# v of the first eight heads loaded in long rows and turned on chip, and the last three second-layer weights loaded in column halves

## The chip, the cores and the metric

The kernel runs on one NeuronCore of a Trainium2 chip. The metric is the device time of one execution in microseconds (us). The work of the core is done by TensorE (PE; its weight loads are listed as PEld), VectorE (DVE), ScalarE (ACT), GpSimd (POOL) and SyncE (SP). The last two are used here almost only to issue DMA transfers, all of which share 16 DMA engines.

## The reference, cut to what matters

An attention over 4 batches of 8 heads (768 positions, head size 64) feeds a soft mixture of experts (3072 tokens of 512 columns, 8 experts of 4 slots, hidden size 1024).

```python
scores = q @ k.T / sqrt(64)              # per batch and head
mask   = causal for retrieval heads; causal and (first 4 keys or last 64) for the others
a      = softmax(where(mask, scores, -1e9))
x      = (a @ v).transpose(0, 2, 1, 3).reshape(3072, 512)

logits = x @ phi                         # 3072 x 32
d = softmax(logits, axis=0); slot_input = d.T @ x        # 32 slots
for e in range(8):
    slot_out[e] = relu(slot_input[e] @ w1[e]) @ w2[e]
c = softmax(logits, axis=1); out = c @ slot_out          # 3072 x 512, float32
```

All inputs are float32 in device memory: q, k and v 6.29 MB each, w1 and w2 16.8 MB each. The output has 6.29 MB.

## The kernel before

**Order of the work.** The program is written with a manual schedule: every engine executes its instructions in the order in which the code issues them. There is no planner. What the code writes first stands first in the queue of its engine.

**Attention, rounds 0 to 15.** The 32 heads are taken as 16 pairs; round n handles pair n (two heads of batch n // 4). One round has six chunks of scores. `scores(n, c)` (L160) multiplies on PE and `exp`s on ACT from PSUM into `pT`. `mask` (L174) multiplies three of the chunks on DVE. `pvmm(n - 1, i)` (L186), which multiplies the exponentials of the pair before with v, stands between the chunks on PE; its products are divided by their sums in `norm` (L196) on DVE. For the pair after this one, `transposes` (L135) turns q and k, 24 transposes of 64x64 each, into PSUM tiles `tpq` and `tpk`; `evac` (L144) copies them to `Tq` (on DVE) and `Tk` (on ACT), and undoes the order in which the rows came. `vfar(n)` (L154) makes on DVE a masked copy of v. Two buffers in PSUM (tag `tr`) serve all transposes in turn: a third waits until the first has been copied away.

**Loads.** Every load casts from float32 to bf16 and is issued by POOL, in the order of the code. `load_qk` (L106) takes q and k so that a partition holds 12 consecutive positions of a head: rows of 12 x 64 floats, 3 KB. `load_v` (L116) puts position p of a block of 128 in partition p, which is the layout that `pvmm` reads: rows of 64 floats. A load of v has four heads and 0.39 MB in bf16. `w_load` (L128) issues the weights in between. A load whose buffer is still in use makes POOL wait; for q and k that ends with the last transpose of the pair that used the buffer before.

**The end of attention and the experts.** The buffers of `w2_5`, `w2_6` and `w2_7` are those of the mask and of `pT`, so these three are loaded only when the last rounds free them (L401 to L441): `w2_5` and `w2_6` whole, `w2_7` in two column halves, left and right. After the last pair the logits, the slot inputs and the first layer follow (L428 to L487). `second(e, xs)` (L507) adds the second layer of expert e to the column halves `xs` of the slots, in two PSUM banks `sp`. Experts 0 to 3 go together, then 4, 5, 6; after that 7 products with zeros keep PE occupied, and `second(7, (0,))` ends the left half:

```python
    second(5, spread=True)
    second(6, spread=True)
    keep_busy(idle, 7)
    second(7, (0,), spread=True)
```

**Outputs.** The tokens are laid out as 24 rows of 128 tokens. `product` (L540) multiplies one row with `slot_out`, and ACT or DVE scales it by the sum of its exponentials. `half_rows` does so for one column half. The left half of rows 0 to 7 (`NL = 8`) is made as soon as the left `slot_out` is there, and written from POOL's queue; then the right half of expert 7 is added, rows 8 to 23 are made whole, and the right half of rows 0 to 7 comes last, both written from SP's queue.

Of the kernel before, what the change touches and what calls it, by code (L numbers as in the profile page):

```python
# [10 lines left out]
F32 = mybir.dt.float32  # L11
BF16 = mybir.dt.bfloat16
# [26 lines left out]
def kernel(  # L39
# [13 lines left out]
    nc = tc.nc  # L53
    P = 128
    B, H, S, D = q.shape
    n_sink, window = int(n_sink), int(window)
    ES = moe_phi.shape[1]
    NE, DM, F = moe_w1.shape
# [11 lines left out]
    xp = ent(tc.tile_pool(name="xp", bufs=2))  # L70
    scp = ent(tc.tile_pool(name="scp", bufs=2, space=PSUM))
    trp = ent(tc.tile_pool(name="trp", bufs=2, space=PSUM))
    pvp = ent(tc.tile_pool(name="pvp", bufs=2, space=PSUM))

    def single(shape, dt, name, tag=None):
        return singles.tile(shape, dt, name=name, tag=tag or name)

    w1s = [single([P, 4, F], BF16, f"w1_{e}") for e in range(NE)]
    w2s = [single([P, 8, DM], BF16, f"w2_{e}") for e in range(NE - 3)] + [None] * 3
    ident = single([P, P], BF16, "ident")  # L80
# [23 lines left out]
    qraw, kraw, qT, kT, vf, pT, pv, xb = {}, {}, {}, {}, {}, {}, {}, {}  # L104

    def load_qk(pairs, order="qk"):  # L106
        b, h, c = pairs[0] // 4, 2 * (pairs[0] % 4), 2 * len(pairs)
        t = raw.tile([P, 2, 2, S], BF16, tag="raw", name="raw")
        for which in order:
# [3 lines left out]
            for x, n in enumerate(pairs):  # L113
                d[n] = t[:, z, x]

    def load_v(m):  # L116
        b, h = m // 2, 4 * (m % 2)
        nc.gpsimd.dma_start(vbs[m % 3].rearrange("p h j d -> p (h j) d")[:, :, :D],  # L118
                            v[b, h:h + 4].rearrange("h (j p) d -> p (h j) d", p=P))

    def vb(n):
        return vbs[n // 2 % 3][:, 2 * (n % 2):2 * (n % 2) + 2]

    w1v = [moe_w1[e].rearrange("(di do) f -> di do f", do=4) for e in range(NE)]
    w2v = [moe_w2[e].rearrange("(fi fo) d -> fi fo d", fo=8) for e in range(NE)]
# [7 lines left out]
            wi[0] += 1  # L133

    def transposes(n, which):  # L135
        src = (qraw if which == "q" else kraw)[n]
        tp = trp.tile([P, 12, 64], BF16, tag="tr", name="tp" + which)
        for s in range(12):
            for hh in range(2):
                po = slice(64 * hh, 64 * hh + 64)  # L140
                nc.tensor.transpose(tp[po, s, :], src[po, 64 * s:64 * s + 64], ident[po, po])  # L141
        return tp

    def evac(n, which, tp):  # L144
        dst = qkT.tile([P, S], BF16, tag="T" + which, name="T" + which)
        o, i = dst.rearrange("c (p s) -> c p s", s=12), tp.rearrange("c s p -> c p s")
        if which == "q":
            nc.vector.tensor_copy(o, i)  # L148
            qT[n] = dst
        else:  # L150
            nc.scalar.copy(o, i)  # L151
            kT[n] = dst

    def vfar(n):  # L154
        h = 2 * (n % 4)
        t = vfp.tile([P, 2, 4, 66], BF16, tag="vf", name="vf")
        nc.vector.tensor_mul(t, vb(n)[:, :, :4, :], fmask[:, h:h + 2])
        vf[n] = t
# [27 lines left out]
    def pvmm(n, i):  # L186
        if i % 3 == 0:
            pv[n] = pvp.tile([P, 3, 2, 65], F32, tag="pv", name="pv")
        for hh in range(2):
            for j in range(i + 1):  # L190
                vv = vb(n) if i - j <= 1 else vf[n]
                o = BLK[j, i]
                nc.tensor.matmul(pv[n][:, i % 3, hh, :], pT[n][:, hh, o:o + 128], vv[:, hh, j, :D + 1],  # L193
                                 start=(j == 0), stop=(j == i))
# [68 lines left out]
    def keep_busy(t, count):  # L263
        for _ in range(count):
            nc.tensor.matmul(t, zero[:, :P], zero, start=True, stop=True)  # L265

    idle = pvp.tile([P, 512], F32, tag="pv", name="idle")
# [52 lines left out]
    for n in range(NP):  # L320
        if n == 0:
            load_qk([2])
            load_v(1)
        elif n == 1:
            load_qk([3])
        elif n == 2 or (n % 2 == 1 and n < 12):
            m = 2 if n == 2 else (n + 3) // 2
            load_qk([2 * m, 2 * m + 1])
            load_v(m)
        w_load(1 + 5 * (n + 1) // 8)  # L330
        if n == 0:
            nc.gpsimd.dma_start(phi, moe_phi.rearrange("(do di) s -> di do s", di=P))
        b, r = n // 4 - 1, n % 4
        last = n - 1

        scores(n, 0)
        if n >= 1:
            for i in range(3):
                pvmm(last, i)
        if b >= 0 and r == 2:  # L340
            logits_mm(b, (0, 1, 2, 3))

        scores(n, 1)
        if b >= 0 and r == 2:
            logits_exp(b)
        if n >= 1:
            norm(last, 0)
        if 0 < n < NP - 1:
            tq = transposes(n + 1, "q")
            evac(n + 1, "q", tq)  # L350
        mask(n, 0)
        if b >= 0 and r == 3:
            exp_tokens(b)

        scores(n, 2)
        if n >= 1:
            pvmm(last, 3)
        if n >= 2:
            x_transpose(n - 2)
        mask(n, 1)  # L360

        scores(n, 3)
        if 0 < n < NP - 1:
            tk = transposes(n + 1, "k")
        mask(n, 2)

        scores(n, 4)
        if 0 < n < NP - 1:
            evac(n + 1, "k", tk)
        if n >= 1:  # L370
            pvmm(last, 4)
        if n:
            vfar(n)

        scores(n, 5)
        if n == 0:
            vfar(0)
        if n >= 1:
            pvmm(last, 5)
            norm(last, 1)  # L380
        if b >= 0 and r == 3:
            dispatch_mm(b)
            slot_sum(b)
        if n == 0:
            evac(1, "q", transposes(1, "q"))
            evac(1, "k", transposes(1, "k"))
        if n < 3:
            far_mask(n + 1)
            for h in (2 * n + 2, 2 * n + 3):
                head_mask(h)  # L390
        elif n == 3:
            setup_late()
# [3 lines left out]
    left, right, full = slice(0, 256), slice(256, 512), slice(0, 512)  # L396

    def w_half(e, cs):
        nc.gpsimd.dma_start(w2s[e][:, :, cs], w2v[e][:, :, cs])

    w2s[5] = single([P, 8, DM], BF16, "w2_5", tag="msk")  # L401
    nc.gpsimd.dma_start(w2s[5], w2v[5])
    w2s[6] = ptp.tile([P, 8, DM], BF16, tag="pT", name="w2_6")
    nc.gpsimd.dma_start(w2s[6], w2v[6])


    def bank(t, shape=(P, 512), dt=F32):
# [30 lines left out]
    logits_mm(bl, (0, 1, 2))  # L438
    w2s[7] = ptp.tile([P, 8, DM], BF16, tag="pT", name="w2_7")
    w_half(7, left)  # L440
    w_half(7, right)  # L441
    x_transpose(last, 0, 3)
    x_transpose(last, 3, 6)
    copies(2, 0)
    idle = bank(2)
# [11 lines left out]
    idle = bank(2)  # L457
# [10 lines left out]
    cs = bank(1, (P, 1))  # L468
# [5 lines left out]
    for e4 in range(2):  # L474
        t = xp.tile([P, 2, 512], BF16, tag="xb", name="hs")
# [29 lines left out]
    idle = spt[1][:, 1]  # L505

    def second(e, xs=(0, 1), spread=False):  # L507
        e4, g = e // 4, e % 4
        for fo in range(8):
            c = fo % 4 if spread else g  # L510
            for x in xs:
                nc.tensor.matmul(sp[x][32 * c:32 * c + 32, :], hT[e4][:, fo, 32 * g:32 * g + 32],  # L512
                                 w2s[e][:, fo, 256 * x:256 * x + 256],
                                 start=(e4 == 0 and fo == 0), stop=(e == 7 and fo >= 4))
# [13 lines left out]
        er.append(e)  # L528
        nc.tensor.matmul(rp[:, r:r + 1], e[:ES], ones[:ES], start=True, stop=True)
    V.reciprocal(rrow, rp)  # L530
    second(5, spread=True)
    second(6, spread=True)
    keep_busy(idle, 7)
    second(7, (0,), spread=True)


    NL = 8
    ov = out.rearrange("(p r) d -> p r d", r=24)

    def product(r, o, cs, t):  # L540
        op = bank(t, (P, cs.stop - cs.start))
        nc.tensor.matmul(op, er[r], slot_out[:, cs], start=True, stop=True)  # L542
        if t == 2:
            nc.scalar.activation(o, op, ACT.Copy, scale=rrow[:, r:r + 1])  # L544
        else:
            V.tensor_scalar(o, op, rrow[:, r:r + 1], None, op0=ALU.mult)  # L546

    def half_rows(cs, t0, groups, banks, eng):
        ot, r = single([P, NL, 256], F32, f"oh{t0}", tag=f"w1_{t0}"), 0
        for rows in groups:  # L550
            for _ in range(rows):
                product(r, ot[:, r], cs, banks[r % len(banks)])
                r += 1
            eng.dma_start(ov[:, r - rows:r, cs], ot[:, r - rows:r])  # L554

    V.tensor_copy(slot_out[:, left], sp[0])  # L556
    half_rows(left, 0, (2, 2, 4), (1, 2), nc.gpsimd)
    second(7, (1,), spread=True)
    V.tensor_copy(slot_out[:, right], sp[1])  # L559
    r = NL  # L560
    for z, groups in enumerate(((1, 1, 2), (4,), (4,), (4,))):
        ot, base = single([P, 4, DM], F32, f"ot{z}", tag=f"w1_{4 + z}"), r
        for rows in groups:
            for _ in range(rows):
                if r == NL:
                    for t, cs in ((1, left), (2, right)):
                        product(r, ot[:, 0, cs], cs, t)
                else:
                    product(r, ot[:, r - base], full, (1, 2)[r % 2])
                r += 1  # L570
            nc.sync.dma_start(ov[:, r - rows:r, :], ot[:, r - rows - base:r - base])
    half_rows(right, 2, (4, 4), (1, 2), nc.sync)


# [33 lines left out]
```

The softmax here doesn't subtract the row's maximum and nothing guards it: scores larger than these inputs give would overflow.

## Time and profile before

| | |
|---|---|
| median of three runs | 159.69 us (159.01 to 160.25) |
| the profiled execution | 159.01 us, of which its span is 157.2 us |
| PE, DVE, ACT, POOL busy | 76%, 67%, 70%, 24% of the span |
| read from device memory, written to it | 52.49 MB, 6.29 MB |
| L172, 96 exponentials on ACT | 83.4 us, 923 ns each |
| L151, 16 copies Tk on ACT | 12.9 us, 804 ns each |
| L148, 16 copies Tq on DVE | 15.3 us, 956 ns each |
| L211, 17 copies xT on DVE | 9.0 us, 529 ns each |
| loads of v, 8 of 384 KB | 13.0 us from issue to landing (median) |
| mean granted clock of PE | 0.921 |

Busy shares are means over stages with different limits. In the page's slices, one character stands for a fortieth of the span (3.93 us), and a 9 for 90% or more. A chain line has a start, a duration, and the engine and line that the time went to. In a timeline the brackets give the idle time of the engine ahead of the instruction and what ended it. A wait is put down to the semaphore that came last.

### The profile page before, as it was taken

What the parts mean: (1) busy time and instruction counts of PE and PEld (TensorE: products, weight loads), DVE (VectorE), ACT (ScalarE), POOL (GpSimd) and SP (SyncE); (2) the same over time, 40 slices, a digit from 0 to 9 for tenths busy, and PEclk for the clock granted to TensorE, in tenths of its full rate; (3) what the DMA queues carried; (4) which work ended last, traced back from release to release, by engine and by line L of the source; (5) the groups of instructions that cost most, each with busy time, mean ns of one, the idle gap of its engine ahead of it and who ended that gap; (6) DMA issues with size and microseconds to landing.
All of it is one profiled execution on the core that took longest, in us unless ns stands there. A gap on an engine that the chain in (4) does not pass through costs nothing. (4 is left out here: it accounts for less than half of the span.)

```text
span 157.2 us, 5051 instructions
## 1 busy us (share of the span) xinstructions
PE 119.3 (76%) x2241; PEld 74.8 (48%) x2243; DVE 105.8 (67%) x245; ACT 109.5 (70%) x147; POOL 38.0 (24%) x54
## 2 busy tenths in 40 slices
PE   6757698868597879977978977978897897788000
PEld 2325466545365555655655655645633673344000
DVE  2886459998986878977869979768724410489000
ACT  3286589969799999999898999899242310389000
POOL 7674051900350350250084100001320000040000
PEclk9975559999999999999999999999999998799955
DMA  3999999999999999999999999999999999369995
GB/s 46 165 186 204 169 217 207 192 190 186 219 215 200 186 217 200 185 224 195 188 213 198 191 219 213 217 215 217 215 217 213 219 196 183 44 226 401 404 387 182
DMA packets 36135, 32.85 MB, mean 209 GB/s; under 512 B 26002, under 2 KB 33170, under 8 KB 33810
## 3 DMA queue, kind: packets, MB, share of 16 engines
q0 software_dynamic: 34192, 27.30, 109.8%
q1 hardware_dynamic: 1922, 5.24, 8.7%
q8 instruction: 17, 0.28, 0.7%
q14 instruction: 4, 0.03, 0.1%
HBM read 52.49 MB, written 6.29 MB: 374 GB/s over the span
## 5 line engine op out<-in xcount | busy, mean ns | idle before, releaser
L172 ACT ACTIVATE pT<-sc 128x1024 bf16<-128x1024 f32 (+1 forms) x96 | 83.4, 923 | 9.4 <-PE sc L167 8.9
L167 PE MATMUL sc<-Tq,Tk 64*128 64x256 bf16 (+3 forms) x320 | 36.6, 292 | 13.4 <-ACT Tk L151 9.8
L193 PEld LDWEIGHTS <-pT 128*128 128x128 bf16 x672 | 25.0, 99 | 12.2 <-issue 7.8
L184 DVE TENSOR_TENSOR pT<-pT,msk 128x1024 bf16<-128x1024 bf16 (+1 forms) x48 | 29.4, 640 | 0.2 <-ACT pT L172 0.2
L193 PE MATMUL pv<-vb,pT 128*128 128x65 bf16 x352 | 27.6, 196 | 0.3 <-DVE xb L202 0.3
L193 PE MATMUL pv<-vf,pT 128*128 128x65 bf16 x320 | 25.4, 198 | 0.0
L167 PEld LDWEIGHTS <-Tk 64*128 64x128 bf16 x320 | 11.2, 95 | 22.5 <-ACT Tk L151 13.1
L141 PEld LDWEIGHTS <-raw 64*64 64x64 bf16 x768 | 15.9, 115 | 10.9 <-issue 7.5
L202 DVE TENSOR_TENSOR xb<-pv,rs 128x384 bf16<-128x384 f32 x32 | 17.8, 557 | 1.1
L148 DVE COPY Tq<-tpq 128x768 bf16<-128x768 bf16 x16 | 15.3, 956 | 4.9 <-PE tpq L141 4.6
L111 POOL DMA_DIRECT2D raw<-in_q_dram x10 | 6.4, 639 | 49.5 <-PE tpk L141 48.3
L151 ACT COPY Tk<-tpk 128x768 bf16<-128x768 bf16 x16 | 12.9, 804 | 4.9 <-PE tpk L141 4.9
L201 DVE RECIPROCAL rs<-pv 128x6 f32<-128x6 f32 x32 | 6.2, 195 | 12.5 <-PE pv L193 12.4
L141 PE MATMUL tpk<-ident,raw 64*64 64x64 bf16 x384 | 9.8, 201 | 2.9 <-DMA raw<-in_k_dram 1.5
L118 POOL DMA_DIRECT2D vb<-in_v_dram x8 | 11.6, 1452 | 1.1 <-issue 0.9
L141 PE MATMUL tpq<-ident,raw 64*64 64x64 bf16 x384 | 9.6, 200 | 1.2 <-DMA raw<-in_q_dram 1.2
L210 PE MATMUL tpx<-ident,xb 128*128 128x128 bf16 x96 | 8.1, 218 | 2.0 <-ACT expT L224 1.1
L211 DVE COPY xT<-tpx 128x768 bf16<-128x768 bf16 (+1 forms) x17 | 9.0, 529 | 0.8 <-PE tpx L210 0.8
L544 ACT ACTIVATE oh<-bank,rrow 128x256 f32<-128x256 f32 x8 | 3.5, 474 | 8.7 <-PE bank L542 8.6
L542 PE MATMUL bank<-slot_out,expR 128*128 128x256 bf16 (+1 forms) x33 | 7.9, 323 | 1.7 <-DVE slot_out L556 0.5
L132 POOL DMA_DIRECT2D w<-in_moe_w_dram x12 | 6.6, 556 | 4.3 <-DMA raw<-in_q_dram 2.6
L554 POOL DMA_DIRECT2D out_dram<-oh x3 | 2.2, 737 | 22.4 <-ACT oh L544 22.4
(88 smaller groups left out, 117.2 us busy)
## 6 DMA issues: line engine op xcount, KB each, us to landing
w<-in_moe_w_dram POOLq DMA_DIRECT2D x15, 1024.0 KB, 18.0
vb<-in_v_dram POOLq DMA_DIRECT2D x8, 384.0 KB, 13.0
out_dram<-ot SPq DMA_DIRECT2D x3, 1024.0 KB, 7.7
raw<-in_q_dram POOLq DMA_DIRECT2D x6, 384.0 KB, 10.0
raw<-in_k_dram POOLq DMA_DIRECT2D x6, 384.0 KB, 11.6
w<-in_moe_w_dram POOLq DMA_DIRECT2D x2, 512.0 KB, 21.8
out_dram<-oh SPq DMA_DIRECT2D x2, 512.0 KB, 9.5
raw<-in_k_dram POOLq DMA_DIRECT2D x4, 192.0 KB, 6.9
```

What stands on the lines that cost most here:

```text
L118: nc.gpsimd.dma_start(vbs[m % 3].rearrange("p h j d -> p (h j) d")[:, :, :D], v[b, h:h + 4].rearrange("h (j p) d -> p (h j) d", p=P))
L141: nc.tensor.transpose(tp[po, s, :], src[po, 64 * s:64 * s + 64], ident[po, po])
L148: nc.vector.tensor_copy(o, i)
L151: nc.scalar.copy(o, i)
L167: nc.tensor.matmul(sc[:, hh, at:at + 128 * cnt], kT[n][po:po + 64, j * 128:(j + 1) * 128], qT[n][po:po + 64, i0 * 128:(i0 + cnt) * 128], s ...
L172: nc.scalar.activation(pT[n][:, :, o:o + ln], sc[:, :, :ln], ACT.Exp, scale=scale)
L184: nc.vector.tensor_mul(x, x, m)
L193: nc.tensor.matmul(pv[n][:, i % 3, hh, :], pT[n][:, hh, o:o + 128], vv[:, hh, j, :D + 1], start=(j == 0), stop=(j == i))
L202: nc.vector.tensor_mul(xb[b][:, 3 * half:3 * half + 3, h * D:(h + 2) * D].rearrange("p i (h d) -> p i h d", h=2), pv[n][:, :, :, :64], rs. ...
L210: nc.tensor.transpose(tp[:, i * 128:(i + 1) * 128], xb[b][:, i, hp * 128:(hp + 1) * 128], ident)
L211: nc.vector.tensor_copy(xT[:, hp, i0 * 128:i1 * 128], tp[:, i0 * 128:i1 * 128])
L542: nc.tensor.matmul(op, er[r], slot_out[:, cs], start=True, stop=True)
```

## The change

The change has two parts.

First, v of pairs 0 to 3 (batch 0) is loaded like q and k, in rows of 12 positions, into a tile `vraw` that shares its buffers with `xb`. The new `v_blocks(n)` turns it twice: 24 transposes of 64x64 on PE (as for q and k), a copy `Tv` on ACT that undoes the order of rows, six transposes of 128x128 on PE, and a copy on DVE into the place from which `pvmm` reads. `v_blocks(0)` stands at the end of round 0, ahead of the transposes of pair 1; `v_blocks(1)` to `v_blocks(3)` stand in rounds 1 to 3 between `pvmm(n - 1, 4)` and `vfar(n)`, ahead of `scores(n, 5)`. The other twelve pairs are loaded as before.

Second, `w2_5`, `w2_6` and `w2_7` all come in column halves, first the three left ones and then the three right ones; the left halves of experts 5, 6 and 7 are added first, without the seven products with zeros, and the right ones after the left output rows. `NL` is 12 instead of 8, and `product` takes its engine from the row's number.

```diff
+    vraw = xp.tile([P, 2, 2, S], BF16, tag="xb", name="vraw")
+
     def load_v(m):
         b, h = m // 2, 4 * (m % 2)
+        if m < 2:
+            nc.gpsimd.dma_start(vraw[:, m], v[b, h:h + 4].rearrange("(y h) (p s) d -> (h p) y (s d)", h=2, s=12))
+            return
         nc.gpsimd.dma_start(vbs[m % 3].rearrange("p h j d -> p (h j) d")[:, :, :D],
...
     def transposes(n, which):
-        src = (qraw if which == "q" else kraw)[n]
+        src = vraw[:, n // 2, n % 2] if which == "v" else (qraw if which == "q" else kraw)[n]
...
             nc.scalar.copy(o, i)
-            kT[n] = dst
+            if which == "k":
+                kT[n] = dst
+            return dst
+
+    def v_blocks(n):
+        vT = evac(n, "v", transposes(n, "v"))
+        tp = trp.tile([P, 6, P], BF16, tag="tr", name="tpv")
+        for j in range(6):
+            nc.tensor.transpose(tp[:, j, :], vT[:, 128 * j:128 * j + 128], ident)
+        nc.vector.tensor_copy(vb(n).rearrange("p h j d -> p j h d")[:, :, :, :D], tp.rearrange("p j (h d) -> p j h d", h=2))
...
         if n >= 1:
             pvmm(last, 4)
+        if 0 < n < 4:
+            v_blocks(n)
         if n:
             vfar(n)
 
         scores(n, 5)
         if n == 0:
+            v_blocks(0)
             vfar(0)
...
     w2s[5] = single([P, 8, DM], BF16, "w2_5", tag="msk")
-    nc.gpsimd.dma_start(w2s[5], w2v[5])
+    w_half(5, left)
     w2s[6] = ptp.tile([P, 8, DM], BF16, tag="pT", name="w2_6")
-    nc.gpsimd.dma_start(w2s[6], w2v[6])
+    w_half(6, left)
...
     w_half(7, left)
-    w_half(7, right)
+    for e in (5, 6, 7):
+        w_half(e, right)
...
-    second(5, spread=True)
-    second(6, spread=True)
-    keep_busy(idle, 7)
-    second(7, (0,), spread=True)
-
-
-    NL = 8
+    for e in (5, 6, 7):
+        second(e, (0,), spread=True)
+
+
+    NL = 12
...
-        if t == 2:
+        if r % 2:
             nc.scalar.activation(o, op, ACT.Copy, scale=rrow[:, r:r + 1])
...
     V.tensor_copy(slot_out[:, left], sp[0])
-    half_rows(left, 0, (2, 2, 4), (1, 2), nc.gpsimd)
-    second(7, (1,), spread=True)
+    half_rows(left, 0, (2, 2, 4, 4), (1, 2), nc.gpsimd)
+    for e in (5, 6, 7):
+        second(e, (1,), spread=True)
     V.tensor_copy(slot_out[:, right], sp[1])
...
-    for z, groups in enumerate(((1, 1, 2), (4,), (4,), (4,))):
+    for t, groups in enumerate(((1, 1, 2), (4,), (4,))):
...
-    half_rows(right, 2, (4, 4), (1, 2), nc.sync)
+    half_rows(right, 2, (4, 4, 4), (1, 2), nc.sync)
```

More of the change, by code (lines that the diff above doesn't have):

```diff
@@ L548, in half_rows @@
     def half_rows(cs, t0, groups, banks, eng):
-        ot, r = single([P, NL, 256], F32, f"oh{t0}", tag=f"w1_{t0}"), 0
+        ots = [single([P, n, 256], F32, f"oh{t0 + x}", tag=f"w1_{t0 + x}") for x, n in enumerate((8, NL - 8))]
+        r = 0
         for rows in groups:
             for _ in range(rows):
-                product(r, ot[:, r], cs, banks[r % len(banks)])
+                product(r, ots[r // 8][:, r % 8], cs, banks[r % len(banks)])
                 r += 1
-            eng.dma_start(ov[:, r - rows:r, cs], ot[:, r - rows:r])
+            eng.dma_start(ov[:, r - rows:r, cs], ots[(r - 1) // 8][:, (r - rows) % 8:(r - 1) % 8 + 1])
     V.tensor_copy(slot_out[:, left], sp[0])
-    half_rows(left, 0, (2, 2, 4), (1, 2), nc.gpsimd)
-    second(7, (1,), spread=True)
+    half_rows(left, 0, (2, 2, 4, 4), (1, 2), nc.gpsimd)
+    for e in (5, 6, 7):
+        second(e, (1,), spread=True)
     V.tensor_copy(slot_out[:, right], sp[1])
     r = NL
-    for z, groups in enumerate(((1, 1, 2), (4,), (4,), (4,))):
-        ot, base = single([P, 4, DM], F32, f"ot{z}", tag=f"w1_{4 + z}"), r
+    for t, groups in enumerate(((1, 1, 2), (4,), (4,))):
+        ot, base = single([P, 4, DM], F32, f"ot{t}", tag=f"w1_{4 + t}"), r
         for rows in groups:
             for _ in range(rows):
[L565 to L569, printed above, removed]
+                product(r, ot[:, r - base], full, (1, 2)[r % 2])
                 r += 1
             nc.sync.dma_start(ov[:, r - rows:r, :], ot[:, r - rows - base:r - base])
-    half_rows(right, 2, (4, 4), (1, 2), nc.sync)
+    half_rows(right, 2, (4, 4, 4), (1, 2), nc.sync)
 _INS = ['q', 'k', 'v', 'is_retrieval', 'n_sink', 'window', 'moe_phi', 'moe_w1', 'moe_w2']
```

## The prediction

> **What bounds the kernel now.** I read the page's slices first, then the chain that ended last, then the timelines of the early rounds and of the end, with windows of a microsecond for the DMA rates.
>
> ```profile
> PEclk9975559999999999999999999999999998799955
> DMA  3999999999999999999999999999999999369995
> GB/s 46 165 186 204 169 217 207 192 190 186 219 215 200 186 217 200 185 224 195 188 213 198 191 219 213 217 215 217 215 217 213 219 196 183 44 226 401 404 387 182
> ```
>
> The DMA engines are full until slice 34, empty in a hole at 132 to 138 us, and full again with outputs. The chain shows what fills the hole:
>
> ```profile
> 110.00 21.41 DMA w<-in_moe_w_dram
> ...
> 131.45 0.63 PE bank L512 x16
> ...
> 132.24 2.57 PE bank L265 x6
> 134.80 0.58 PE bank L512 x8
> ...
> 135.41 0.44 DVE slot_out L556
> ```
>
> The 21.41 us are not one transfer but the queue before it. After w2_6 lands, PE runs 2.57 us of zero products, then the left half of expert 7; the left slot_out starts at 135.41. The first output bytes follow 2.8 us later (the windows view has 0 GB/s at 137 to 138 and 172 at 138 to 139), and the last leave at about 155.4. So the end is set by the time of that slot_out plus the writing of 6.29 MB. The compute chain is little behind the data: PE ran expert 5 at 129.82 without a wait for data and waited 1.00 us for expert 6.
>
> The rounds ahead of that are bound by ACT (nearly 100% from 44 us on), except for a few gaps early (timeline, all engines; start, duration, engine, and in brackets the idle time before and what ended it):
>
> ```profile
> 8.32 5.06 ACT L172 ACTIVATE pT<-sc 128x1024 bf16<-128x1024 f32 x6 [1.06 <-PE sc L167]
> ...
> 17.85 0.85 PE L141 MATMUL tpq<-ident,raw 64*64 64x64 bf16 x24 [1.19 <-DMA raw<-in_q_dram]
> ...
> 23.34 0.20 DVE L201 RECIPROCAL rs<-pv 128x6 f32<-128x6 f32 x1 [1.63 <-PE pv L193]
> ...
> 27.68 1.02 ACT L172 ACTIVATE pT<-sc 128x1024 bf16<-128x1024 f32 x1 [0.28 <-PE sc L167]
> ...
> 28.60 0.79 ACT L151 COPY Tk<-tpk 128x768 bf16<-128x768 bf16 x1
> ...
> 29.28 4.21 ACT L172 ACTIVATE pT<-sc 128x512 bf16<-128x512 f32 x5
> ...
> 32.07 0.95 DVE L148 COPY Tq<-tpq 128x768 bf16<-128x768 bf16 x1
> ...
> 33.87 0.57 PE L141 MATMUL tpk<-ident,raw 64*64 64x64 bf16 x24 [1.45 <-DMA raw<-in_k_dram]
> ...
> 41.47 1.02 ACT L172 ACTIVATE pT<-sc 128x1024 bf16<-128x1024 f32 x1 [0.86 <-PE sc L167]
> ```
>
> The reader is to see two waits for data, 1.19 us in round 1 and 1.45 us in round 3. The second is nearly false: the same transposes need the buffer that DVE's Tq copy frees at 33.02, so without the wait for k they could begin 0.85 us sooner and no more. The line at 23.34 is where DVE, having waited for PE, starts the chain that ends in such a Tq copy. The gap of round 4 (0.86 on ACT) is DVE's, not data's.
>
> [...] 163 GB/s at 17 to 20 us, where v moves in 64-element rows, against a mean of 213 with weights alone (92 to 120 us). [...] Here the granted clock is 0.50 from 10 to 23 us, so the first turn is paid at half clock. [...] Tk stands between two exponentials every round.
>
> **The change part by part.**
>
> *v in long rows.* A load of 0.393 MB at 163 GB/s takes 2.41 us, at the 205 GB/s that q, k and weights make together at 24 to 30 us 1.92: twice 0.5 = 1.0 us of DMA time (0.6 to 1.5). POOL's issue falls from 1.42 to about 0.70 us; POOL is idle. This pays only if DMA stays the bound.
>
> *The turns.* v_blocks puts on PE 24 small transposes (0.57 at full clock), on ACT a copy of Tk's shape (0.80), on PE 6 transposes (0.49), on DVE a copy (0.53 as xT's, 0.96 as Tq's). PE waits for ACT in the middle, and behind it on PE stand scores(n,5), for which ACT waits in turn. Taken at round 2: Tk ends 29.39, the v copy about 30.10, the six end 30.62, scores(2,5) 30.78, its exponential 0.63, then exp(3,0) at 31.56 instead of 29.91 (29.28 plus one of 0.63): 1.65 us.
>
> *Turn 0* stands before the transposes of pair 1. v's 24 start at 12.36, end 13.2; ACT is in exponentials until 13.38, copies to 14.18; six at half clock (0.8) to 15.0; k's transposes need the buffer that the DVE copy frees at 15.6 to 16.0, then 0.85, Tk 0.80: scores(1,0) at 17.3 to 17.7 instead of 14.74. +2.8. It hides the q wait of round 1 in full: -1.2.
>
> *Turn 1*: +1.9 (1.7 to 2.3, by the clock); [...] -0.3.
>
> *DVE behind the turns.* The copy (0.53 to 0.96) and vfar (0.43) now come after the six transposes and ahead of rs, xb, fmask, msk, rs, xb, Tq, the transposes of k and scores(n,4). In round 2 that chain began 0.47 before exp(2,0) and now begins 0.02 to 0.45 after it; ACT was already waiting for it (the 0.28), so +0.7. In round 3 it began 0.82 before; now Tq ends at what was 33.9 to 34.3, which takes the place of the data wait: +0.2 (0 to 0.4). In round 4, with setup_late in the chain, it began 1.1 before and ACT already lost 0.86: +1.3 (1.1 to 1.6).
>
> *Turns 2 and 3*: +1.65 each.
>
> Sum until round 4: 2.8 - 1.2 + 1.9 - 0.3 + 0.7 + 1.65 + 0.2 + 1.65 + 1.3 = 8.7 us (7.7 to 10.3). No later round waits for data, so the delay reaches the end of the attention part (110.05) and PE's second product of expert 5: 129.8 + 8.7 = 138.5.
>
> *Halves of w2_5 and w2_6.* At 128 to 132 us, where w2_7's 512 B pieces mix in, 196 GB/s against 213: 5.35 for 4.92 us, +0.4 each (0 to 0.6). POOL issues two more DMAs at 0.89 us; idle. Covered by the compute delay: raw loads wait for PE's transposes, so their issue is late too and DMA runs dry for 1 to 2 us about four times from 32 us on. I put the inputs' end at 140 to 142, before the first output (142.4). If that cover is gone it costs what it is late, up to 2 us.
>
> *Zero products and order of the second products.* 7 x 0.43 of work and the wait for w2_7's left half go. From 138.5 all left halves are there (w2_7 left by about 133): 24 products, 0.95 by the 0.63 of 16, and 0.3 for the last to end, so that without any delay the cast would start at 131.1 instead of 135.41: -4.3. The right half's 24 products come after the left products, another 0.95, with 12 left rows (1.57 MB, 3.9 us) being written meanwhile; full rows are ready about 6 us after the left cast, the left ones are drained at 6.9. No starved start (before, 1.3 us of bytes were lost at 138 to 141): -0.6. Eight more half rows in 1 KB pieces, 1.05 MB at 343 (153 to 155 us) rather than 405 GB/s: +0.5. Two more products and evictions at 0.2 lie beside writing. Tail: -4.4 (-3.8 to -5.0).
>
> **Sum.** +8.7 - 4.4 = +4.3 on the profiled 159.01 us (span 157.2 and 1.8 around it): 163.3. That run is the lowest of three, 0.7 below the median of 159.69; I leave the number as it is, since the three spread over 0.8%. About 1% is what can be told from no change.
>
> **Rivals.**
> - *The DVE copies hide.* If DVE's chain has slack in rounds 2 to 4, 2.2 us go: d = 6.3 with a tail of -4.6 gives 160.7. For it: DVE is at 67%. Against: ACT waits in exactly those places already. 0.16.
> - *Faster: the turns fit into the waits.* If PE and ACT do v's turn wholly in time in which they wait (1.06, 0.71, 1.44, 1.31 us idle on ACT before 35 us), d is about 2 and the left half is ready 2.4 us sooner than now: 156.6. It decides from d below 4.4. For it: PE is at half load and DMA still full at 35 us; earlier q and k help. Against: the waits of ACT in those rounds are partly its own chain, and turns 2 and 3 have none beside them. 0.13.
> - *The clock stays at half.* [...] six more half-speed gaps of 0.3 and slower turns, +2.7: 166.0. For it: the clock fell at 9.8 in just such a round. Against: round 1 is dense once q is there. 0.09.
>
> **How the numbers follow.** The forecast holds 0.62, at 163.3, own range 161.0 to 165.3. Slower by over 1%: 0.60 from it, 0.03 of the DVE rival, 0.09 of the clock: 0.72. Within 1%: 0.02, 0.13 and 0.01 of the fast rival: 0.16. Faster: 0.12. The range, 158.5 to 166.0, takes forecast and DVE rival whole and half the clock's.
>
> **What would show it.** Right: four Tv copies of 0.80 on ACT; no q wait in round 1; exp(4,0) at about 44.4 (now 37.0); the last exponential ending near 118.7; DMA gaps near 33 and 50 us; the left slot_out at 139.8; outputs without a hole after 142.5; span 161.5. Wrong: exp(4,0) before 41.4, or a left slot_out before 135.4, which would make it faster; an input end after 143 would mean that DMA, not the rounds, decides.

## The result and the profile after

The changed kernel takes 164.64 us (median of six, 164.07 to 165.18) against 159.03 for the kernel before on the same chip: a ratio of 1.033, 95% interval 1.029 to 1.037, so 3.3% slower. Medians here and below are of all executions of a kernel; the ratios and their intervals leave out those that ran over 1.5% above its fastest. Of the 5.0 us between the two spans (157.2 and 162.2) the trace makes two parts: the attention rounds end 9.0 us later, and what follows them is 4.0 us shorter. The forecast had 8.7 and 4.4.

The page of the changed kernel (slices: granted clock, share of the DMA engines, GB/s), and then the pieces of its chain of waits at the end:

```profile
PEclk9955576986995999999999999999999999999655
DMA  3999999999996997999999999999999999979995
GB/s 47 161 218 199 183 221 175 179 176 153 218 212 122 188 207 134 187 196 186 187 199 162 180 198 206 216 224 210 210 226 202 192 199 196 177 237 367 410 360 186
```

```profile
138.88 0.80 PE bank L531 x24
...
139.70 0.43 DVE slot_out L574
...
142.64 0.80 PE bank L531 x24
...
143.46 0.43 DVE slot_out L578
```

The DMA engines are no longer full in the middle: slices 12 and 15 have 122 and 134 GB/s, where raw loads (q and k) were issued late. The chain no longer holds a wait for weights. The 24 products of the left halves run at once; the left slot_out starts at 139.70 (forecast 139.8; 135.41 before).

What became of the rounds, in ACT's timeline (brackets: idle time before, and what ended it):

```profile
13.28 0.82 ACT L157 COPY Tv<-tpv 128x768 bf16<-128x768 bf16 x1
...
18.01 1.02 ACT L187 ACTIVATE pT<-sc 128x1024 bf16<-128x1024 f32 x1 [0.70 <-PE sc L182]
...
24.20 0.82 ACT L157 COPY Tv<-tpv 128x768 bf16<-128x768 bf16 x1
26.07 0.60 ACT L187 ACTIVATE pT<-sc 128x512 bf16<-128x512 f32 x1 [1.05 <-PE sc L182]
27.44 1.02 ACT L187 ACTIVATE pT<-sc 128x1024 bf16<-128x1024 f32 x1 [0.77 <-PE sc L182]
...
33.02 0.83 ACT L157 COPY Tv<-tpv 128x768 bf16<-128x768 bf16 x1
34.68 0.60 ACT L187 ACTIVATE pT<-sc 128x512 bf16<-128x512 f32 x1 [0.82 <-PE sc L182]
35.54 2.17 ACT L187 ACTIVATE pT<-sc 128x1024 bf16<-128x1024 f32 x2 [0.26 <-DVE vf L172]
...
44.47 3.56 ACT L187 ACTIVATE pT<-sc 128x1024 bf16<-128x1024 f32 x4 [0.26 <-DVE vf L172]
50.22 1.02 ACT L187 ACTIVATE pT<-sc 128x1024 bf16<-128x1024 f32 x1 [2.19 <-PE sc L182]
```

After the copies Tv of rounds 1 to 3 the next exponential, that of chunk 5, has to wait 0.82 to 1.05 us for PE: its scores stand behind the six transposes, which could start only when Tv was there. And the gap before exp(4,4), the line at 50.22, has grown from 0.86 to 2.19 (exp(n,c) is the exponential of chunk c in round n). The groups of the turn say the same from PE's side (busy, mean ns, idle before):

```profile
L166 PE MATMUL tpv<-ident,Tv 128*128 128x128 bf16 x24 | 2.5, 250 | 5.8 <-ACT Tv L157 5.8
L167 DVE COPY vb<-tpv 128x768 bf16<-128x768 bf16 x4 | 2.2, 558 | 10.4 <-PE tpv L166 10.4
```

PE stood still for 5.8 us waiting for the four copies Tv. That is more than it worked on the 24 transposes of 128x128 (2.5).

The starts of exp(n,0) set the steps of the forecast beside what happened:

| start of | before | changed | later by | forecast | split turns (below) |
|---|---|---|---|---|---|
| exp(1,0) | 15.39 | 18.01 | 2.6 | 2.8 | 2.8 |
| exp(2,0) | 23.84 | 27.44 | 3.6 | 3.2 | 2.3 |
| exp(3,0) | 29.93 | 35.54 | 5.6 | 5.55 | 3.1 |
| exp(4,0) | 37.05 | 44.47 | 7.4 | 7.4 | 3.3 |
| exp(5,0) | 43.72 | 52.69 | 9.0 | 8.7 | 3.8 |
| end of the last exponential | 110.05 | 119.04 | 9.0 | 8.7 | 4.4 |

### The profile page after: what moved, and what is told of

Read it like the earlier page. It is cut to its first block, busy times and chain, and to the rows that moved or that the text cites. A ratio compares the mean times of both kernels' runs of the same rounds, so it can differ in the third digit from the quotient of the medians.

```text
span 162.2 us, 5297 instructions
## 1 busy us (share of the span) xinstructions
PE 123.2 (76%) x2357; PEld 79.7 (49%) x2359; DVE 108.1 (67%) x251; ACT 113.2 (70%) x152; POOL 39.4 (24%) x57
## 5 line engine op out<-in xcount | busy, mean ns | idle before, releaser
L182 PE MATMUL sc<-Tq,Tk 64*128 64x256 bf16 (+3 forms) x320 | 38.0, 303 | 11.0 <-ACT Tk L157 7.7
L208 PEld LDWEIGHTS <-pT 128*128 128x128 bf16 x672 | 25.9, 101 | 12.8 <-issue 8.1
L208 PE MATMUL pv<-vb,pT 128*128 128x65 bf16 x352 | 28.5, 200 | 0.3 <-DVE xb L217 0.3
L208 PE MATMUL pv<-vf,pT 128*128 128x65 bf16 x320 | 26.0, 201 | 0.0
L417 POOL DMA_DIRECT2D w<-in_moe_w_dram x6 | 5.2, 878 | 27.1 <-PE pv L208 25.3
L124 POOL DMA_DIRECT2D vb<-in_v_dram x6 | 8.5, 1422 | 4.3 <-PE pv L208 3.6
L167 DVE COPY vb<-tpv 128x768 bf16<-128x768 bf16 x4 | 2.2, 558 | 10.4 <-PE tpv L166 10.4
L561 ACT ACTIVATE oh<-bank,rrow 128x256 f32<-128x256 f32 x12 | 5.2, 472 | 4.0 <-PE bank L559 3.9
```

Of the source, the lines that this page charges most:

```text
L182: nc.tensor.matmul(sc[:, hh, at:at + 128 * cnt], kT[n][po:po + 64, j * 128:(j + 1) * 128], qT[n][po:po + 64, i0 * 128:(i0 + cnt) * 128], s ...
```

## The experiments

The theory is the forecast's: a turn costs the rounds more than its instructions, since PE waits in its middle and DVE's work comes late after it; the tail gains; DMA time is not what decides. The rivals put the loss into the halved weights, or the cost into the work itself.

**The first part alone.** The first part of the diff on the kernel before, without the second.

```diff
+        if 0 < n < 4:
+            v_blocks(n)
...
     w_half(7, left)
     w_half(7, right)
...
     keep_busy(idle, 7)
```

> The first part of the change alone: v of pairs 0 to 3 in long rows and turned; the weights, products and outputs at the end as before. Theory (the turns delay the rounds, about 9 us, and nothing takes it up later): the second product of expert 5 at 138.8 as in the changed kernel, then 0.63 for expert 6, the seven zero products (1.5 at full clock, 2.6 at half) and 0.3 for expert 7, so the left slot_out at 142 to 143 against 135.4 before: 6.6 to 7.7 us slower, about 166. Rival (the loss lies in the halved weights and in DMA at the end): within 1 us of before, about 159 to 160.

Measured: 1.046 times the kernel before (1.035 to 1.057), 7.3 us slower at its 159.9. That is within the theory's 6.6 to 7.7, though the interval is wider (5.5 to 9.0 us). Where the left slot_out came was not seen: the one profiled execution took 199.19 us, with slower products on PE (two zero products in 0.89 us, 0.54 in the changed kernel; six of them in 3.05, 2.57 in the kernel before), and is not read. The first part is the loss, all of it.

**The second part alone.** `v_blocks`, `vraw` and the case of `load_v` taken out of the changed kernel.

```diff
-        if m < 2:
-            nc.gpsimd.dma_start(vraw[:, m], ...)
-            return
...
-        if 0 < n < 4:
-            v_blocks(n)
```

> The second part of the change alone: w2_5, w2_6 and w2_7 in column halves, no zero products, 12 split rows; v loaded as before. Theory: expert 5 at 129.8 as before, the left slot_out at about 131 to 132 instead of 135.4, left rows written while the right halves end: 3 to 4.5 us faster, about 155. Rival (half columns cost the DMA engines what they bring, at 0.4 to 0.6 us a weight, and the inputs' end near 137 holds the right half back): at most 1 us faster, 158 to 159; if the halves were the loss, slower than 160.

Measured: 157.07 us, ratio 0.987 (0.976 to 0.997): 2.2 us faster by the ratio, less than the 3 to 4.5 of the theory and more than the rival's 1 us at most. Its chain and windows tell why (windows: after the length, busy time of PE, PEld, DVE, ACT and POOL, then clock, DMA share and GB/s):

```profile
115.10 22.10 DMA w<-in_moe_w_dram
...
137.91 0.43 DVE slot_out L560
```

```profile
138.00:139.00 1.00, 0.61 (x2) 0.31 (x2) 0.33 (x1) 0.00 (x0) 0.00 (x0) 0.50 0.75 295
139.00:140.00 1.00, 0.78 (x2) 0.33 (x2) 0.89 (x2) 0.57 (x1) 0.00 (x0) 0.50 0.35 135
140.00:141.00 1.00, 1.00 (x4) 0.43 (x3) 0.90 (x2) 0.81 (x2) 0.00 (x0) 0.50 0.39 145
```

The left slot_out was at 130.11, 5.3 us sooner than before, but the right one stayed at 137.91 (137.88 before): the last right half landed at 137.2, after PE had waited 2.04 us for it. That is the rival's reason, though the gain is larger than it allowed. Most of the 12 left rows were written by 139, and the DMA engines had 135 and 145 GB/s until whole rows came. With nothing late ahead of it, the tail is DMA's, and its gain is what the left rows fill.

**The long rows without the turns.** The loads of v in long rows, ones in place of v of pairs 0 to 3, the end as before.

> The long rows without the turns, the end as before. Left out: v of pairs 0 to 3 is loaded into its tile and not used, ones stand in its place. Theory (two loads of v are 0.5 us of DMA time shorter each, and the inputs decide the end): q of pair 2 comes up to 1 us sooner, and the end is 1.0 us earlier (0.6 to 1.5): about 158. Rival (DMA time is not what decides, the rounds are): no change, 159.0, within 0.3 us.

Measured: 157.56 us, ratio 0.988 (0.980 to 0.995), 2.0 us faster. The chain of waits no longer has a transfer of weights among its last pieces, and PE goes through experts 5 and 6 without a stop:

```profile
128.94 1.84 PE bank L528 x32
...
131.11 2.00 PE bank L280 x6
133.10 0.36 PE bank L528 x8
133.49 0.43 DVE slot_out L572
```

Before, expert 6 waited 1.00 us for its weights. The gain is above the theory's 1.0 (0.6 to 1.5), and the rival's "no change" is out. From 130 us on 0.57 MB of input are still to come, where before it was 0.83 (sums of the windows), about 1.3 us of DMA time by an estimate at 200 GB/s (the windows of before have 190 and 206 at 130 to 132 us). The rounds, which now wait less for q of pair 2 (0.76 on ACT against 1.44), end 1.0 sooner. And of the 1.9 us by which the left slot_out comes sooner in this trace, about 0.8 are zero products and products of expert 7 that ran less at half clock (2.00 and 0.36 us against 2.57 and 0.58; granted clock 0.91 at 132 to 133 us and 1.00 at 133 to 134, against 0.71 and 0.50); that has nothing to do with v. So the long rows by themselves are worth having, and the turns are what they cost; how the 2.0 divide was not separated.

**The turn in two places.** The changed kernel, with the first half of turns 1 to 3 moved up.

```diff
+        if 0 < n < 4:
+            v_first(n)              # 24 transposes, Tv
         if n >= 1:
             pvmm(last, 3)
...
         if 0 < n < 4:
-            v_blocks(n)
+            v_second(n)             # six transposes, copy on DVE
```

> The changed kernel with the turns of pairs 1 to 3 in two places: the 24 transposes and ACT's copy Tv already after scores(n, 2), the six transposes and DVE's copy where they were, so that PE does not stand still between the two halves and ACT has its exponential when Tv ends. Same instructions. Theory (half of a turn's cost is PE waiting for ACT, 1.65 us a turn of which 0.8 is the copy itself): 0.8 less for each of three turns and up to 0.5 less of DVE's lateness: 2.4 to 3.5 us faster than the changed kernel, about 161.5. Rival (the work itself, ACT's 0.8 and DVE's copy, costs it): less than 1 us faster, about 164.

Measured: 160.34 us, ratio 1.003 (0.999 to 1.008) to before, with the same instructions, where the changed kernel has 1.033 (measured in another set of runs): 4.3 us less by the medians, 4.8 by the ratios. More than the 2.4 to 3.5 expected; the rival (the work itself, less than 1 us) is out. ACT's timeline:

```profile
28.63 0.82 ACT L157 COPY Tv<-tpv 128x768 bf16<-128x768 bf16 x1
29.82 1.94 ACT L191 ACTIVATE pT<-sc 128x1024 bf16<-128x1024 f32 x2 [0.37 <-PE sc L186]
...
42.28 2.81 ACT L191 ACTIVATE pT<-sc 128x1024 bf16<-128x1024 f32 x3 [0.86 <-PE sc L186]
45.29 1.02 ACT L191 ACTIVATE pT<-sc 128x1024 bf16<-128x1024 f32 x1 [0.20 <-PE sc L186]
```

The wait behind Tv in round 2 falls from 0.82 to 0.37, and the long gap of round 4, ahead of exp(4,4) (the line at 45.29), from 2.19 to 0.20. (The 0.86 is another gap, ahead of exp(4,1).) The clock differs too. Its line on the page:

```profile
PEclk9975559999999999999999999999999999779955
```

Between 22 and 60 us the mean granted clock is 0.98 here, as before, and 0.87 in the changed kernel (0.90 in its second profile). There it fell to 0.50 at 25.3 to 28.7, 35.6 to 39.0 and 49.2 to 52.6 us, the first two times just after PE had stood still in a turn, the third after PE's wait of 1.99 us for Tq in round 4 (last section); here none of these falls is left. How much of the gain is clock and how much the waits themselves was not separated. One pair of traces gives an idea: after turn 1 the clock fell in the changed kernel (mean granted clock of the profile 0.894) and stayed up in the first profile of the next experiment (0.919), and the gaps ahead of exp(1,5) and exp(2,0) are 1.05 and 0.77 us in the one, 0.82 and 0.27 in the other.

**setup_late moved.** In the changed kernel, the 2.2 us of small DVE work stand in round 0.

```diff
         if n == 0:
+            setup_late()
             v_blocks(0)
...
-        elif n == 3:
-            setup_late()
```

> The changed kernel with one move: setup_late, 2.2 us of small work on DVE, stands in round 0 ahead of v_blocks(0), where DVE was idle for 3.4 us waiting for the six transposes, instead of after round 3. Theory (the gap of 2.19 us on ACT in round 4 is DVE's chain of vb copy, vfar, norm, setup_late, norm and Tq, made later by the turn): that gap falls to 0.3 or less, 1.8 to 2.2 us faster than the changed kernel, about 162.7. Rival (the gap is PE's half clock or the turn of q itself): less than 0.5 us.

The first set of runs left it open: 164.30 us in the median, 161.44 to 166.1, too far apart to compare. A second set had the changed kernel beside it:

> The changed kernel with setup_late in round 0, a second time: its profiled run had lost the 2.19 us gap of round 4 and was 3 us shorter than the changed kernel's, but its timed runs lay between 161.4 and 166.1. Theory (DVE's lateness is a term of its own): 1.5 to 2.5 us faster than the changed kernel in the median. Rival (what the gap gives is taken back by PE's clock or by a later wait): within 0.5 us of it.

> The changed kernel once more, so that the three beside it are compared with it on the same chip. About 164 to 165, as before; its PE clock fell to half after each turn, and if that varies from run to run its time does so too, within 2 us.

Measured on one chip: the changed kernel 164.66, with the move 162.99; ratios to before 1.034 and 1.024. That is 1.7 us, within the theory's 1.5 to 2.5. In both profiles with the move the gap ahead of exp(4,4) is gone (from the second):

```profile
45.09 4.76 ACT L187 ACTIVATE pT<-sc 128x1024 bf16<-128x1024 f32 x5 [0.76 <-PE sc L182]
```

Five exponentials, exp(4,0) to exp(4,4), run without a pause. So the wait in round 4 is DVE's, and it is a term of its own. What the turn added to it is not shown by this run: with setup_late gone from the chain, the 0.86 us that the kernel before lost there go too. Nor does the gap always have the same size: in the second profile of the changed kernel it is 0.76, and another of 1.28 stands ahead of exp(3,4), where PE waited 1.42 us for DVE's Tq.

**Half of the turns.** Only pairs 0 and 1, or only pairs 2 and 3, in long rows; the condition in `load_v` and in the rounds changed to match.

```diff
-        if m < 2:
+        if m == 0:                  # or m == 1
...
-        if 0 < n < 4:
+        if n == 1:                  # or 1 < n < 4, and no v_blocks(0)
```

> The changed kernel with only pairs 0 and 1 in long rows and turned; pairs 2 and 3 as before. Theory (the costs add up, and only the first turns stand beside a wait for data): exp(2,0) 3.6 us later than before as in the changed kernel, some 0.5 more from DVE in round 2, and round 3 gives back 0.9 to 1.3 of its wait for k: about 3.3 us of delay, the left slot_out at 133.5, 157.5 to 158.5 in all. Rival (the delay is one per kernel, whatever the number of turns): 162 or more.

> The changed kernel with only pairs 2 and 3 in long rows and turned, rounds 0 and 1 as before. Theory (1.65 us for each of turns 2 and 3, 0.2 of DVE's lateness in round 3 and 1.3 in round 4, nothing hidden): about 4.8 us of delay, the left slot_out at 135, 158.8 to 160 in all. With the run of pairs 0 and 1 the two delays should add up to the 9.0 of the changed kernel within 1 us. Rival (turns in rounds bound by ACT hide in DVE's and PE's spare time): within 1 us of the second part alone, 157 to 158.

Measured: 159.97 us (1.002, 0.998 to 1.006) and 161.33 (1.015, 1.007 to 1.022), both above what was expected. The last exponential ends 5.0 and 5.4 us later than before, against 3.3 and 4.8. Together 10.4, where the changed kernel has 9.0 and, in its second profile, 9.4: they add up within 1.0 to 1.4 us, where 1 was expected, so the costs belong to the turns and are not one delay per kernel, nor do turns in rounds bound by ACT hide. With turns 2 and 3 alone, 0.7 of the 5.4 us are there at exp(2,0), ahead of the first turn; the rest is 4.7, about what was expected. With turns 0 and 1 alone, exp(5,0) is 2.9 late, near the 3.3 expected, and exp(6,0) is 5.0 late. The rounds between them ran in part at half clock:

```profile
PEclk9995576899975899999999999999999999999755
```

This is the kernel with turns 0 and 1. Its clock was at half from 45.55 to 52.37 us, three rounds after its last turn. Ahead of that stands the gap of round 4, 1.16 us on ACT ahead of exp(4,4) at 44.20; the last section returns to it.

**The zero products alone.** Taken out of the kernel before.

```diff
-    keep_busy(idle, 7)
```

> The kernel before without the seven zero products ahead of expert 7's left half, nothing else. Theory (the zeros outlast the landing of w2_7's left half): left slot_out at 133.7 to 134.5 instead of 135.4, right one about 1 us sooner: 1.0 to 1.5 us faster than before. Rival (PE would wait for the left half as long as the zeros take): no change within 0.3 us; [...]

Measured: 158.80 us, ratio 1.001 (0.998 to 1.004). No change, as the rival has it: without the zeros PE waited for the left half of w2_7, which landed at 134.2, and the left slot_out came at 134.90 instead of 135.41. In the kernel before that half had landed at about 134.1 and the zeros ended at 134.80, so most of them lie inside a wait for data; the 0.5 us gained on the left half earned nothing, as the right slot_out stayed where it was (137.94, 137.88 before).

**Two tries for a faster version.** The second part alone, with `NL = 16` and one more group of four left rows:

> The second part of the change alone, with 16 split rows in place of 12. In the run with 12 the DMA engines fell to 135 and 145 GB/s at 139 to 141 us: the 12 left rows were written before the first whole rows were there. Theory (the hole is want of left rows): four more left rows, 0.5 MB, fill it; 0.8 to 1.3 us faster than with 12, about 156. Rival (the landing of the last right half at 137.2 and the slower 1 KB pieces set the end): within 0.3 us of it.

Measured: 156.33 us, ratio 0.984 (0.979 to 0.989), the fastest of all; it beats both kernels. The hole is filled:

```profile
139.00:140.00 1.00, 0.78 (x3) 0.45 (x3) 0.73 (x1) 0.30 (x1) 0.00 (x0) 0.50 1.02 381
140.00:141.00 1.00, 1.00 (x3) 0.39 (x3) 0.80 (x3) 0.83 (x2) 0.00 (x0) 0.50 0.86 326
```

The span fell by 0.6 us (155.1 to 154.5). The intervals of the ratios with 12 and 16 rows overlap, so that the difference between these two is not shown by the times, and the theory's 0.8 to 1.3 is not confirmed. Then the same with v of pairs 2 and 3 in long rows, the turns split and setup_late in round 1:

> The second part of the change with 16 split rows, and of v only pairs 2 and 3 in long rows, each turned in two places as in the split kernel, with setup_late in round 1 where DVE waits. Theory (the first turn costs most, since it stands ahead of everything of pair 1; a split turn costs 0.8 of ACT; one load of v saves 0.8 to 1.0 of DMA time): the rounds end 0.5 to 1.5 us later than before, covered by the queue of weights, and the end is DMA's: 0.3 to 1.0 us faster than the second part with 16 rows, about 155.5. Rival (any delay of the rounds reaches the end): 0.5 to 1.5 us slower than it.

Measured: 156.87 us, ratio 0.987 (0.982 to 0.991): no gain from the long rows. The last input landed 0.8 us sooner than in the kernel without turns, but the rounds ended at 111.44, 1.4 later, and the left slot_out came at 132.75 (130.72 without the turns), so that the outputs were not ready when the DMA engines were:

```profile
134.00:135.00 1.00, 1.00 (x6) 0.60 (x4) 0.96 (x3) 0.95 (x3) 0.28 (x1) 0.50 0.82 111
```

That the turns took what the load gave is not shown, though. Of the 1.4 us, 1.0 is there already at exp(2,0) (25.30 against 24.28), ahead of the first turn: q of pair 2 came later in this execution, with 2.63 us of waiting on ACT against 1.62.

## Why the prediction was right

The direction, the place of the loss and its size were forecast: 9.0 us lost in the rounds for 8.7, 4.0 won back in the tail for 4.4. Term by term the agreement is less good, and in three places it was luck.

- **Turn 0, +2.8, and the wait for q, -1.2.** 2.6 at exp(1,0). The q transposes of pair 2 had no wait for data in round 1. As reckoned, PE, ACT and DVE passed v from one to the next while pair 1 stood behind.
- **Turn 1, +1.9, and -0.3 for the clock.** exp(2,0) is 3.6 late for 3.2. The -0.3 was the author's estimate, not worked out from a trace. The clock did rise sooner, at 21.9 us instead of 23.2, but it had also fallen sooner (8.26 for 9.55), and stood at half for 13.7 us in both kernels, so that it rose sooner was luck. And it fell again at 25.3, which was not forecast.
- **1.65 for each of turns 2 and 3, DVE's lateness beside them.** Rounds 2 and 3 added 2.0 and 1.8, for 2.35 and 1.85. Here two errors cancel in part. From the end of Tk to exp(n + 1,0) it takes 2.38 us in both rounds, and 0.54 before: a turn costs 1.84, of which the last 0.26 is a wait that the profile puts down to DVE's `vf`. So DVE's chain beside it cost 0.2 and nothing, for 0.7 and 0.2. The changed kernel has no gap ahead of exp(2,4), most likely since PE at half clock (0.50 until 28.74 us) had held ACT up before it: exp(2,0) had waited 0.77 us for it and exp(2,1) 0.24. In the first profile with setup_late moved, where the clock stayed up in that round, the DVE gap is there (0.63).
- **Round 4, +1.3.** The gap was forecast as 0.86 and 1.3, 2.16; it is 2.19 in this profile and 0.76 in the second one, where round 3 lost more instead. The run with setup_late moved shows that the wait is DVE's; that its size is met so closely is luck.
- **No later round gives anything back.** 9.0 at exp(5,0), 9.0 at the last exponential.
- **DMA in cover.** It ran dry from the middle on, and the last right half landed at 142.9, just inside the 143 that the forecast named as the sign against it (143.3 in the second profile). PE did not wait for it in either: in the first, expert 5's right half started at 142.57, straight after the left products. The first part cost the rounds so much that the DMA time it saved was worth nothing, as forecast; the run without turns shows what it would have been worth.
- **Tail, -4.4.** It is -4.0: 4.7 to the left slot_out (from the last exponential 20.66 instead of 25.36, forecast 4.3) and 0.7 back from there to the end, where the forecast had 0.1 more to win. The step that was off is "no starved start": 98 and 85 GB/s at 141 to 143 us, while the last inputs ran out and the first left rows were made. The second part alone shows that the 4.7 is not worth its size by itself: with the rounds in time the left slot_out gains 5.3 us and the end 2.2, since the right half waits for its weights.
- **The rivals.** "The DVE copies hide" is out with 9.0 us of delay for its 6.3, though in rounds 2 and 3 most of DVE's lateness did hide. "The turns fit into the waits" failed at turns 2 and 3 and at PE's place in the middle. "The clock stays at half" came true in part and in another way: not through round 2, but for 3.4 us at a time, after two of the turns and after the wait of round 4. (In the trace before, the clock fell at 9.55 us, not at 9.8 as this rival has it.) The own range of the forecast, 161.0 to 165.3, holds the measured 164.64; the forecast of 163.3 is 1.3 us low, of which 0.7 lies in the spans (162.2 for 161.5).

## What to carry to other kernels

A turn through two engines is priced by the order in which its parts stand in the queues: the same instructions cost half as much (4.4 us at the last exponential for 9.0) once the first half stood early enough that PE no longer stood still for its copy; the mean granted clock between 22 and 60 us was 0.98 for 0.87, and its part of the gain was not separated. A round that waits for data hides work only up to that wait, and the next constraint, here a DVE chain that ended 0.85 us earlier, may lie just under it. Shorter transfers pay only where the engines that use them are not made later by as much; price both before the change. And one trace is one draw: a gap of 2.19 us was 0.76 in the next profile of the same kernel.

## What was not expected of the hardware

The granted clock fell to 0.50 inside busy rounds. In the profile of the changed kernel it was at half from 25.33 to 28.74, from 35.57 to 38.98 and from 49.22 to 52.64 us. The stretch ahead of the first fall, the stretch at half clock after it, and the stretches ahead of the second and the third fall (windows as above: PE's busy time after the length, the clock third from the end):

```profile
21.91:25.33 3.42, 1.82 (x61) 1.41 (x58) 0.82 (x2) 3.11 (x4) 2.79 (x3) 1.00 1.03 212
25.33:28.74 3.41, 3.41 (x45) 1.99 (x44) 2.85 (x9) 1.66 (x3) 0.06 (x1) 0.50 1.00 169
32.15:35.57 3.42, 1.72 (x34) 1.18 (x31) 1.26 (x4) 2.34 (x5) 0.68 (x2) 1.00 1.48 166
45.81:49.22 3.41, 1.42 (x37) 1.06 (x35) 3.25 (x13) 2.21 (x3) 0.00 (x0) 1.00 1.02 214
```

Each of the three stretches ahead of a fall has a wait of PE in it: 1.60 us for Tv in turn 1, 1.70 us for Tv in turn 2, 1.99 us for Tq in round 4. But turn 3 stopped PE for 1.60 us as well, like turn 1, until 42.84, and the clock stayed at 1.00 until 49.22; so it did not fall after each turn, as the expectation for the second profile has it. In the kernel with turns 0 and 1 the fall at 45.55 came after the gap of 1.16 us in round 4. And in the kernel without the zero products the clock went from 0.99 at 129 to 130 us to 0.50 at 130 to 131, with PE busy for 3.73 of the 4 us from 126 to 130 (24 of the products there were one column wide).

Two executions differ as well: after the same turn 1 the clock fell at 25.33 us in the first profile of the changed kernel and stayed up in the first one with setup_late moved. What decides between a fall and none was not shown.
